# One row per partition of w_down's second part, loaded in four transfers behind wo

## The chip, the cores and the metric

The kernel runs on one core of one Trainium2 chip. The metric is the time of one execution on the device in microseconds (us); less is better. A comparison takes the median of several executions.

## The reference

One decoding step (one token) of a transformer block in bf16: a layernorm, attention with grouped queries over a long cache, the output projection, a second layernorm and a gated feed-forward network, with two residual additions.

```python
B, Sq, D = 1, 1, 1024
Hq, Hkv, Sk, Dh = 32, 4, 65536, 128
F = 3584
...
def _B_ref(x, w_gate, w_up, w_down):
    return (_gelu(x @ w_gate) * (x @ w_up)) @ w_down

x = A_x
h = x + _A_ref(_layernorm(x, axis=-1), A_k_cache, A_v_cache, A_wq, A_wo)
h2 = h + _B_ref(_layernorm(h, axis=-1), B_w_gate, B_w_up, B_w_down)
```

`_A_ref` multiplies by wq, takes the softmax of the scaled scores against k_cache, sums v_cache with it, and multiplies by wo. The caches hold 2 x 64 MB, the weights some 38 MB, and each byte is used once, for a single token.

## The kernel before

The program streams 173 MB through a ring of four slots in SBUF (`ring`, 32 KB per partition and slot). All large transfers are issued by SP, in the order in which the program lists them: wq in two halves (slots 0 and 1), then for each of eight steps (four key-value heads, two halves of the sequence) two K pieces of 4 MB (slots 2 and 3) and one V piece of 8 MB (slots 0 and 1), then wo (8 MB, slots 2 and 3), w_gate (7 MB, slots 0 and 1), w_up (7 MB, slots 2 and 3), and w_down (7 MB, slots 0 and 1). A transfer into a slot waits until PE is done with what the slot held: wo for the last score matmul (`done`), gate for the last matmul on V (`s_step`), up for the matmuls on wo, w_down for those on gate. These waits stand on SP; what SP has issued is worked off by 16 DMA engines in order.

The order is written out by a small recorder, `Flow`. `op` notes an engine's instruction with the tiles that it reads (`r`) and writes (`w`), `dma` a transfer, and `issue` (line 76) emits all of them with the semaphore waits that these need; so most instructions of the profile have line 95 or 91. `dma` returns the count that a semaphore has when the transfer has landed (16 more for each transfer); with `inc` it is left to the reader to wait for that count. The loop over the attention steps on PE (lines 415 to 449) stands apart from it.

w_down has F = 3584 rows of 1024 numbers (2048 bytes). The first P x FA = 2048 rows are its first part, 16 rows on each of 128 partitions (`wa`, slot 0). The other 1536 rows are its second part, FB = 12 rows per partition (`wb`, slot 1), loaded in three pieces of 8, 3 and 1 rows per partition. `parts` lists the four pieces with the semaphore and the count that PE waits for: `r_sem[0]` for the first part, `r_sem[1]`, `k_sem[0]` and `k_sem[1]` for the three pieces. A row per partition is used by eight matmuls of 128 columns (`down`, line 590), whose stationary operand is one column of the activations `actz`. All of them add into two banks, which hold h as their starting value. Ahead of the first part and ahead of the second part's first piece, `stay_busy(4)` runs four matmuls on data that is thrown away (line 598). After the last matmul, DVE and ACT copy the two banks (lines 607 and 608), and SP stores the output (line 609).

Of the kernel before, what the change touches and what calls it, by code (L numbers as in the profile page):

```python
# [11 lines left out]
BF16 = mybir.dt.bfloat16  # L12
# [4 lines left out]
class Flow:  # L17
# [13 lines left out]
    def op(self, e, call, r=(), w=(), after=(), wait=(), inc=None, dma=False, rows=None, **kw):  # L31
        i = len(self.ops)
        deps = {}

        def need(j, hard):
            o = self.ops[j]
            if o["e"] == e and not dma and not o["dma"] and (e == "pe" or not hard):
                return
            deps[j] = True

        for k in r:
            if k in self.writer:
                need(self.writer[k], True)
        for k in tuple(w) + tuple(after):
            if k in self.writer:
                need(self.writer[k], True)
            for j in self.readers.get(k, ()):
                need(j, False)
        if e == "pool":
            if self.rows[0] != rows and self.rows[1] is not None and not self.ops[self.rows[1]]["inc"]:  # L50
                deps[self.rows[1]] = True
            self.rows = rows, i
        last = {}
        for j in deps:
            o = self.ops[j]
            k = j if o["dma"] else o["e"]
            last[k] = max(last.get(k, j), j)
        deps = last.values()
        for k in r:
            self.readers.setdefault(k, []).append(i)  # L60
        for k in w:
            self.writer[k] = i
            self.readers[k] = []
        self.ops.append(dict(e=e, call=call, kw=kw, deps=sorted(deps), wait=wait, inc=inc, dma=dma))
# [44 lines left out]
def kernel(  # L109
# [14 lines left out]
    P = 128  # L124
    D = A_x.shape[-1]
# [4 lines left out]
    F = B_w_gate.shape[1]  # L130
# [28 lines left out]
    def sb(name, shape, dtype=F32):  # L159
        return const.tile(shape, dtype, name=name)  # L160
# [9 lines left out]
    def over(offset, shape, dtype=F32):  # L170

        n = 1
        for x in shape:
            n *= x
        if dtype == F32:
            v = kt_bytes[:, offset // 4:offset // 4 + n]
        else:
            v = kt_bytes[:, offset // 4:offset // 4 + n // 2].bitcast(BF16)
        if len(shape) == 2:
            v = v.rearrange("p (a b) -> p a b", a=shape[0])  # L180
        return v

    def slot(i, n=1):
        return ring[:, i * CW:(i + n) * CW]

    f = Flow(nc, tc)
# [5 lines left out]
    r_sem = [tc.alloc_semaphore("r_landed_%d" % i) for i in range(3)]  # L192
# [306 lines left out]
    FA = CW // D  # L499
    FB = FC - FA  # L500
    at_ps = bank[6][:]
    wv = slot(2, 2).rearrange("p (c n) -> p c n", c=Hq)
    f.dma("sp", wv, A_wo.rearrange("(p c) n -> p c n", p=P), w=["R2", "R3"], wait=done, sem=r_sem[2])
    for c in range(Hq):
        for s in range(DS):
            q = 2 * (c % 2) + s
            op("pe", "matmul", r=["o2z", "R2", "R3"], w=["B6"], out=at_ps[32 * q:32 * q + 32, :], lhsT=o2z[:, c, :],
               rhs=wv[:, c, :].rearrange("k (p s c) -> k s p c", s=DS, c=C4)[:, s], start=(c < 2), stop=(c >= Hq - 2), tile_position=(0, 32 * q))
# [62 lines left out]
    actz = over(16384, [FC, 2 * AZ + 2], BF16)  # L571
# [4 lines left out]
    FZ = 4  # L576
    wa = slot(0)[:, 0:FA * D].rearrange("p (e n) -> p e n", e=FA)
    wb = slot(1)[:, 0:FB * D].rearrange("p (e n) -> p e n", e=FB)
    wb_src = B_w_down[P * FA:F, :].rearrange("(p e) n -> p e n", p=P)
    parts = [(wa, 0, FA, f.dma("sp", wa, B_w_down[0:P * FA, :].rearrange("(p e) n -> p e n", p=P), after=["R0"], inc=(r_sem[0], 16)), r_sem[0])]  # L580
    e0 = 0
    for i, z in enumerate((FB - FZ, FZ - 1, 1)):
        part = wb[:, e0:e0 + z, :]
        s = (r_sem[1], k_sem[0], k_sem[1])[i]
        parts.append((part, FA + e0, z, f.dma("sp", part, wb_src[:, e0:e0 + z, :], after=["R1"] if i == 0 else [], inc=(s, 16)), s))
        e0 += z
# [3 lines left out]
    def down(a_row, w_row):  # L590
        for j in (0, 4, 1, 5, 2, 6, 3, 7):
            q, m = divmod(orow[j], 32)
            nc.tensor.matmul((d_ps, d_odd)[q // 2][32 * q:32 * q + 32, :], lhsT=a_row[:, AZ - m:AZ - m + 32], rhs=w_row[:, j * OB:(j + 1) * OB],
                             start=False, stop=False, skip_group_check=True, tile_position=(0, 32 * q))

    def stay_busy(n):
        for i in range(n):
            nc.tensor.matmul(bank[5][:], lhsT=qs[:, 0, 0, 0:P], rhs=qs[:, 1 + i % 3].rearrange("p s c -> p (s c)")[:, 0:NB], start=True, stop=True)

    with tc.tile_critical(no_gpsimd_drain=True):  # L600
        for w_rows, a0, n, at, sem in parts:
            stay_busy({0: 4, FA: 4}.get(a0, 0))
            nc.tensor.wait_ge(sem, at)
            for e in range(n):
                down(actz[:, a0 + e, :], w_rows[:, e, :])
    h2 = sb("h2", [P, 2, OB], BF16)
# [33 lines left out]
```

## Time and profile before

| | |
|---|---|
| median of 3 runs | 409.87 us (409.83 to 410.06) |
| profiled execution, its own time | 409.71 us |
| its span, first to last instruction | 407.8 us |
| mean granted TensorE clock | 0.778 |
| PE, DVE, ACT, POOL busy | 58%, 50%, 10%, 5% of the span |
| wo: issued, last landing | 329.99, 353.82 us |
| w_gate: issued, last landing | 343.84, 370.76 us |
| w_up: issued, last landing | 360.48, 387.72 us |
| w_down, first part: issued, last landing | 377.01, 397.44 us |
| w_down, second part, three pieces: last landings | 402.34, 404.19, 404.81 us |

Times within the profile count from the start of the span; the profiled execution's own time is 1.9 us longer than its span. Engines are PE (matmul), PEld (its weight loads), DVE, ACT, POOL and SP; a q behind the name is the engine's sequencer, which waits and issues. A row of the timeline has its start, its length, the engine, the line, the operation, what it writes and reads, the count, and in brackets the idle time of the engine before it and what ended that. A row of the table by stretches has the stretch, its length, PE's busy time and matmuls, the granted share of the clock, the busy share of the DMA engines, and GB/s. The trace also holds each DMA packet (start, duration, bytes, queue), without the engine's number, and each increment of a semaphore by a DMA: for a transfer of 128 partitions 16 of them, one from each DMA engine. A transfer has landed with the last of these.

### The profile page before, as it was taken

Reading aid. Unit: us, or ns where it says so; the run is one execution under the profiler, and the core shown is the slowest. Engines: PE = TensorE matmul, PEld = TensorE weight load, DVE = VectorE, ACT = ScalarE, POOL = GpSimd, SP = SyncE. Lnnn points to the kernel's source line nnn. Section 1 sums busy time; section 2 is a strip of 40 time slices with the busy share of each in tenths; the row PEclk is TensorE's granted clock in tenths of the full one; section 3 lists DMA queues with packets and bytes.
Section 4 is the critical chain, followed back from the end, with each engine's and each line's share of the span. In section 5 each row is a group of like instructions: output and inputs, shape, how many; then the busy total and the mean of one; then the engine's idle time right before and its main releaser. Section 6 shows DMA issues by size and latency. Waiting matters only on the chain. (4 is left out here: it accounts for less than half of the span.)

```text
span 407.8 us, 3909 instructions
## 1 busy us (share of the span) xinstructions
PE 234.8 (58%) x1645; PEld 105.8 (26%) x1647; DVE 202.5 (50%) x174; ACT 39.5 (10%) x141; POOL 19.2 (5%) x39
## 2 busy tenths in 40 slices
PE   0433855585577368734973686557465747365376
PEld 0211322232232133212321232223132223142324
DVE  1218860876089328924781687089508941010210
ACT  1000003000300300030003000300220021000000
POOL 4210000001000000010000001000000000012000
PEclk9955995599569967978796689689976976565668
DMA  8999999999999999999998999999999999999995
GB/s 344 427 421 452 415 460 411 460 418 412 453 460 418 411 425 488 418 408 421 476 437 376 453 424 444 421 460 418 411 453 466 418 418 424 452 440 435 399 413 220
DMA packets 4815, 173.12 MB, mean 424 GB/s; under 512 B 580, under 2 KB 584, under 8 KB 840
## 3 DMA queue, kind: packets, MB, share of 16 engines
q1 hardware_dynamic: 4760, 173.02, 98.5%
q8 instruction: 5, 0.08, 0.1%
q14 instruction: 2, 0.02, 0.0%
q10 hardware_dynamic: 48, 0.00, 0.0%
HBM read 173.02 MB, written 0.00 MB: 424 GB/s over the span
## 5 line engine op out<-in xcount | busy, mean ns | idle before, releaser
L95 DVE STREAM_TRANSPOSE ktb<-ring 128x4096 f32<-128x4096 f32 x32 | 141.1, 4418 | 83.4 <-DMA ring<-in_A_k_cache_dram 83.4
L427 PE MATMUL bank<-ktb,qs 128*128 128x512 bf16 x512 | 132.6, 418 | 61.3 <-PEq L413 61.3
L427 PEld LDWEIGHTS bank<-ktb,qs 128*128 128x128 bf16 x512 | 51.5, 104 | 139.2 <-issue 93.6
L439 PE MATMUL bank<-ring,pt 128*32 128x512 bf16 x512 | 46.3, 541 | 36.5 <-PEq L413 36.5
L95 ACT ACTIVATE pt<-sc,nb 128x256 bf16<-128x256 f32 x64 | 31.5, 494 | 255.3 <-DVE nb L95 255.3
L439 PEld LDWEIGHTS bank<-ring,pt 128*32 128x32 bf16 x512 | 19.4, 131 | 60.2 <-issue 57.3
L95 DVE STREAM_TRANSPOSE sc<-bank 128x512 f32<-128x512 f32 x32 | 22.2, 695 | 24.6 <-PE bank L427 24.6
L95 PE MATMUL bank<-ring,xz 128*32 128x512 bf16 (+1 forms) x192 | 19.2, 587 | 17.2 <-DMA ring<-in_B_w_gate_dram 5.2
L95 DVE TENSOR_REDUCE mx<-sc 128x8 f32<-128x1536 f32 (+1 forms) x16 | 19.5, 1219 | 0.5
L95 DVE STREAM_TRANSPOSE ktb<-bank 128x512 f32<-128x512 f32 (+1 forms) x6 | 4.0, 672 | 31.3 <-PE bank L95 30.9
L95 POOL COPY qs<-qsel 32x128 bf16<-32x128 bf16 x16 | 7.8, 490 | 231.4 <-PE bank L427 216.8
L95 PEld LDWEIGHTS bank<-ring,xz 128*32 128x32 bf16 x192 | 7.5, 141 | 26.9 <-issue 15.9
L95 ACT ACTIVATION_READ_ACCUMULATOR pt<-sc,nb 128x1 f32 x64 | 12.0, 187 | 0.0
L448 PE MATMUL bank<-sel,acc_sb 128*128 128x8 f32 x64 | 8.2, 255 | 6.2 <-PEq L413 6.2
L431 PE MATMUL bank<-ident_f,mx 128*8 128x128 f32 x8 | 2.2, 269 | 14.6 <-PEq L413 14.6
L448 PEld LDWEIGHTS bank<-sel,acc_sb 128*128 128x128 f32 x64 | 7.7, 191 | 10.0 <-issue 10.0
L95 PE MATMUL bank<-ring,ktb 128*32 128x512 bf16 x64 | 6.4, 586 | 5.9 <-DMA ring<-in_A_wo_dram 5.9
L95 ACT COPY acc_sb<-bank 128x512 f32<-128x512 f32 x8 | 4.7, 586 | 48.9 <-PE bank L439 48.9
L95 DVE TENSOR_TENSOR h_col<-bank,x_col 128x8 f32<-128x8 f32 x1 | 0.2, 167 | 14.8 <-PE bank L95 14.8
L95 PE MATMUL bank<-sel,ktb 128*128 128x16 f32 (+1 forms) x24 | 5.2, 356 | 3.5 <-DVE bank L95 2.7
L95 POOL MEMSET ktb<- 128x1024 bf16 (+2 forms) x3 | 3.5, 1164 | 75.8 <-PE bank L427 75.8
L433 PE MATMUL bank<-diag,ones_f 8*128 8x8 f32 x16 | 3.7, 299 | 5.7 <-PEq L413 5.7
(85 smaller groups left out, 60.9 us busy)
## 6 DMA issues: line engine op xcount, KB each, us to landing
ring<-in_A_k_cache_dram SPq DMA_DIRECT2D x16, 4096.0 KB, 24.9
ring<-in_A_wq_dram SPq DMA_DIRECT2D x2, 4096.0 KB, 16.7
ring<-in_B_w_gate_dram SPq DMA_DIRECT2D x1, 7168.0 KB, 26.9
ring<-in_B_w_up_dram SPq DMA_DIRECT2D x1, 7168.0 KB, 27.2
ring<-in_B_w_down_dram SPq DMA_DIRECT2D x1, 4096.0 KB, 20.4
ring<-in_B_w_down_dram SPq DMA_DIRECT2D x1, 2048.0 KB, 25.0
ring<-in_B_w_down_dram SPq DMA_DIRECT2D x1, 768.0 KB, 25.9
ring<-in_B_w_down_dram SPq DMA_DIRECT2D x1, 256.0 KB, 26.0
```

Source lines behind the costliest of these rows:

```text
L95: ins = getattr(self.eng[e], o["call"])(**o["kw"])
L427: m = nc.tensor.matmul(bank[c][:], lhsT=qs[:, jt].rearrange("p s c -> p (s c)")[:, s * P:(s + 1) * P], rhs=mv[:, :, J, :, u], start=(s == ...
L431: nc.tensor.transpose(out=mxT_ps, in_=mx1[:], identity=ident_f[:]).then_inc(s_step, 1)
L433: nc.tensor.matmul(bc_ps, lhsT=ones_f[0:rep, :], rhs=diag[:], start=True, stop=True).then_inc(s_step, 1)
L439: m = nc.tensor.matmul(acc[32 * q:32 * q + 32, :], lhsT=pt[:, c, n, :, :].rearrange("p h s -> p (h s)"), rhs=v_sb[:, c, :, n, :], start=(c ...
L448: m = nc.tensor.matmul(o_ps, lhsT=acc_sb[:, u * Dh:(u + 1) * Dh], rhs=sel[:, u:SQ:NS], start=(u == 0), stop=(u == NS - 1))
```

## The change

One of the twelve rows per partition of w_down's second part (the first, `wb_src[:, 0]`) goes into a tile of its own, `c_row`, in four transfers of 25, 25, 64 and 14 partitions. They are issued by SP right behind wo and ahead of gate, wait for nothing (the tile is used for nothing else), and count on `r_sem[1]`. The first piece in the ring then has 7 rows instead of 8, and the piece's wait on PE covers the four transfers too, since it waits for the count of all that was issued on `r_sem[1]`. PE runs the eight matmuls of the row in `c_row` behind that wait, ahead of the seven.

```diff
     f.dma("sp", wv, A_wo.rearrange("(p c) n -> p c n", p=P), w=["R2", "R3"], wait=done, sem=r_sem[2])
+    wb_src = B_w_down[P * FA:F, :].rearrange("(p e) n -> p e n", p=P)
+    c_row = sb("c_row", [P, 1, D], BF16)
+    for p0, p1 in ((0, 25), (25, 50), (50, 114), (114, P)):
+        f.dma("sp", c_row[p0:p1], wb_src[p0:p1, 0:1, :], inc=(r_sem[1], 16))
     for c in range(Hq):
...
     wb = slot(1)[:, 0:FB * D].rearrange("p (e n) -> p e n", e=FB)
-    wb_src = B_w_down[P * FA:F, :].rearrange("(p e) n -> p e n", p=P)
     parts = [(wa, 0, FA, f.dma("sp", wa, B_w_down[0:P * FA, :].rearrange("(p e) n -> p e n", p=P), after=["R0"], inc=(r_sem[0], 16)), r_sem[0])]
-    e0 = 0
-    for i, z in enumerate((FB - FZ, FZ - 1, 1)):
+    e0 = 1
+    for i, z in enumerate((FB - FZ - 1, FZ - 1, 1)):
...
         for w_rows, a0, n, at, sem in parts:
-            stay_busy({0: 4, FA: 4}.get(a0, 0))
+            stay_busy({0: 4, FA + 1: 4}.get(a0, 0))
             nc.tensor.wait_ge(sem, at)
+            if a0 == FA + 1:
+                down(actz[:, FA, :], c_row[:, 0, :])
             for e in range(n):
                 down(actz[:, a0 + e, :], w_rows[:, e, :])
```

## The prediction

> **What bounds the kernel now.** I read four views in this order: the page's first three parts, the DMA issues, the PE timeline of the last 12 us, and the granted clock in that stretch. The page's slices of DMA time and its queue table come first:
>
> ```profile
> DMA  8999999999999999999998999999999999999995
> ...
> q1 hardware_dynamic: 4760, 173.02, 98.5%
> ...
> HBM read 173.02 MB, written 0.00 MB: 424 GB/s over the span
> ```
>
> The 16 DMA engines are busy in 98.5% of the span, from the first slice to the last. SP issues gate at 343.84, up at 360.48 and w_down at 377.01 us, each while the transfer before it is still moving (wo lands at 353.82, gate at 370.76, up at 387.72). There is no hole into which the moved rows could go: the change moves no byte less, and what it moves ahead delays gate, up and the first part of w_down by its own time.
>
> The end, in the timeline of PE and of the two copies:
>
> ```profile
> 397.48 3.40 PE L593 MATMUL bank<-ring,ktb 128*32 128x128 bf16 x128
> 401.05 0.81 PE L598 MATMUL bank<-qs 128*128 128x512 bf16 x3 [0.16 <-issue]
> 402.38 0.62 PE L593 MATMUL bank<-ring,ktb 128*32 128x128 bf16 x30 [0.53 <-DMA ring<-in_B_w_down_dram]
> 403.50 1.65 PE L593 MATMUL bank<-ring,ktb 128*32 128x128 bf16 x66 [0.49 <-issue]
> ...
> 404.85 0.12 PEld L593 LDWEIGHTS bank<-ring,ktb 128*32 128x32 bf16 x8 [0.28 <-DMA ring<-in_B_w_down_dram]
> 405.34 0.26 ACT L608 CAST h<-bank 64x128 bf16<-64x128 f32 x1 [26.20 <-PEq L600]
> 405.34 0.28 DVE L607 CAST h<-bank 64x128 bf16<-64x128 f32 x1 [9.89 <-PEq L600]
> 405.71 0.35 SPq L609 DMA_DIRECT2D out_dram<-h  x1
> ```
>
> PE waits for each of the three pieces of w_down's second part, and its last eight matmuls start when the last piece has landed; 0.5 us later the copies run. So **the last landing sets the end**, and a landing is complete only when the slowest of 16 DMA engines is. The trace's landing events, one for each engine, show how uneven these are (us):
>
> ```
> last piece of w_down, 16 engines:
> 402.97 403.09 403.09 403.10 403.14 403.17 403.24 403.32
> 403.35 403.47 403.76 404.29 404.51 404.65 404.67 404.81
> ```
>
> Ten engines are done by 403.47; five are 0.8 to 1.3 us behind them. The trace shows where the lag begins. Packets of the kind "instruction" (16 KB at 33.22, 358.00, 376.88 and 401.08 us, about 1.0 us each; 8 KB at 99.83 and 143.25, 0.3 us each) each sit on one engine, and from each on one more landing lags by 0.4 to 1.4 us and never catches up. The trace does not number the engines, so **which of the 16 lag is the unknown of this case.**
>
> **The change, step by step.** Data packets have these durations: 2048 B takes 84 ns (median of 128), 6144 B 234, 16384 B 615, 32768 B 1213; a 4 B completion mark 9 ns.
>
> 1. *Taken off the second part.* Its first piece has eight packets per engine, which shrink from 16384 to 14336 B. On the line between 6144 and 16384 B (381 ns for 10240 B), a packet goes from 615 to 539 ns: 8 x 0.076 = 0.61 us less on every engine.
>
> 2. *Added behind wo.* 128 packets of 2048 B, unevenly spread. Rows on how: transfers of 128 partitions have 16 landings; x_in's 32 partitions give 16 marks behind 32 packets, two each; the output's four rows give one landing event at 406.17 and four more at 406.86 to 406.90, that is four engines with a row each. All splits are even. Kept even, 64 rows are four on each of 16 engines and 14 rows one on each of 14. For 25 the ends are all 25 on one engine and two on most of them; even and between them is five on each of five, and that I take, with both transfers on the same five. The five then get 5+5+4+1 = 15 rows, nine get 5, two get 4. With marks: 15 x 0.084 + 4 x 0.009 = 1.30 us on the five, 5 x 0.084 + 0.018 = 0.44 on the nine, 4 x 0.084 + 0.009 = 0.35 on the two.
>
> [...]
>
> 3. *Net at the last landing.* The five: +1.30 - 0.61 = +0.69 us. The nine: -0.17. The two: -0.26.
>
> 4. *The queue.* SP issues wo at 329.99 and is free until gate at 343.84; four issues at 0.33 to 0.88 us each (the four of w_down span 2.24) end near 333. They wait for nothing of their own, wo is already ahead of them in each engine's queue, and the engines are busy with V until 334.47. Cost nothing, with ten microseconds of cover.
>
> 5. *What moves in between.* Gate, up and w_down's first part land 0.35 to 0.44 later where the lagging engine is outside the five. The next transfer is issued when PE has finished the one before (377.01, nearly 9 us before up begins to land at 385.85), so a shift of 0.44 opens no hole. The matmuls and the layernorm shift with their data: PE is 0.44 later at the start of w_down.
>
> 6. *PE at the end.* The eight matmuls per row are the same 224, with the row of the new tile ahead of the other seven; no instruction more. The wait at r_sem[1] now covers five transfers; behind it stand the last 96 matmuls and the copies. The four matmuls that keep PE busy then reach from 396.79 into the half-clock stretch, where two or three of them take 0.43 instead of 0.22, so the first part's matmuls start near 398.1 instead of 397.48 (the data lands at 397.88). About 92 of them run at 27 ns until 400.54 and 36 at 14 ns, to 401.1; with the 0.4 and four times 0.22 that follow, PE is ready near 402.3. The first piece lands at 402.34 - 0.17 = 402.17. So the 0.5 us by which PE was ahead there are used up, but not more: 64 matmuls with the 0.5 idle that the timeline shows among them end near 404.0, when the next piece lands (404.02), and the last lands at 404.64.
>
> **Sum**: the last landing goes from 404.81 to 404.64, the copies and the output follow: -0.17 us. The profiled execution took 409.71 us around a span of 407.8, so it would take 409.54; it lies 0.16 under the median of the runs shown, 409.87, which gives 409.70. I forecast **409.7 us**, within 0.2% (0.82 us, about what a measurement of this kernel can tell from no change).
>
> **The rivals.**
>
> *A lagging engine is among the five* (chance 0.22). Then it lands 0.69 later than now. The five laggards end at 404.29, 404.51, 404.65, 404.67 and 404.81, so the last landing would be 404.98 to 405.50: slower by 0.17 to 0.69, 410.0 to 410.6. It decides from one such engine on. [...]
>
> *The memory side of each engine is what is full* (0.10). Every engine moves 32768 B in 1213 ns, 27.0 GB/s, all alike; no row says whether that limit is the engine's or that of the partitions it writes. If it is the partitions', the moved rows cost the same time wherever they are queued: 128 x (84 - 76) / 16 = 0.06 us plus marks, 409.95.
> [...]
>
> *PE becomes the bound* (0.08): slower. The clock in the last stretches:
>
> ```profile
> 397.13:400.54 3.41, 3.41 (x118) 0.50 0.93 396
> 400.54:403.95 3.41, 2.23 (x90) 1.00 0.74 294
> ```
>
> Full clock comes after a stretch in which PE was busy throughout. If a 0.44 to 1.3 us later start leaves that stretch short of full, the half clock lasts on: the first part's 128 matmuls end at 401.5, the four fillers take 1.7 instead of 0.9 and end at 403.6, 64 matmuls at 27 ns reach 405.3 and the last 32 406.2, where now they end near 405.0: +1.2 us, 411.1. In an execution whose clock already falls so, the end is PE's today (405.5) and the change costs 0.6. It decides when the clock after 400.5 is half.
>
> *All 25 rows on one engine* (0.04): the change doesn't spread as meant. That engine gets 55 rows, 4.6 us, -0.61: +4.0. Not a laggard (403.0 to 403.5), it would land near 407.3: 412.4.
>
> **How the numbers follow.** Forecast 0.50 (409.6 to 409.8), the four rivals 0.44, something else 0.06. The forecast's error is mostly one of sign, and all but two cases stay inside 0.2%. Faster by over 0.2% would need four times what can be taken off the laggards: 0.04 for what I do not see. Slower by over 0.2%: all of the single-engine case, half of PE's, and a little of the first: 0.10. Within: 0.86. The range from 409.5 to 410.6 holds the forecast, the laggard among the five and the memory side, and leaves out most of the last two.
>
> **What would show it.** In the changed kernel's landing events, c_row's second 25 rows should have five late events and the others at once; the first piece's packets should take 539 ns; gate should land 0.35 to 0.44 later (1.3 if a laggard is in the five); the last piece's slowest landing should come 0.17 before that of now, with ten landings spread up to 404.2. The forecast is wrong if the last landing moves later, if PE's eight last matmuls no longer start at the landing, or if the clock after 400.5 us is half.

## The result, and the profile after

The changed kernel takes 411.23 us (median of 8 runs, 411.03 to 411.59) against 409.91 us of the kernel before (8 runs, 409.74 to 410.06): a ratio of 1.0032, 95% interval 1.0022 to 1.0043. It is **slower by 1.3 us**, where 0.2 us less was forecast. The profiled execution is the slowest of the eight, 411.59 us with a span of 409.6.

The page shows nothing of it: the DMA engines' share is the 98.5% of before, and the rate falls by 2 GB/s.

```profile
DMA  8999999999999999999999998999899999999995
...
q1 hardware_dynamic: 4928, 173.02, 98.5%
...
HBM read 173.02 MB, written 0.00 MB: 422 GB/s over the span
```

The timeline of PE, with the first copy as its last row, has more:

```profile
355.20 6.11 PE L95 MATMUL bank<-ring,ktb 128*32 128x512 bf16 x64 [6.72 <-DMA ring<-in_A_wo_dram]
373.12 5.21 PE L95 MATMUL bank<-ring,xz 128*32 128x512 bf16 x64 [6.50 <-DMA ring<-in_B_w_gate_dram]
399.70 2.62 PE L596 MATMUL bank<-ring,ktb 128*32 128x128 bf16 x128
402.25 1.04 PE L601 MATMUL bank<-qs 128*128 128x512 bf16 x4
403.99 0.30 PE L596 MATMUL bank<-c_row,ktb 128*32 128x128 bf16 x8 [0.70 <-DMA ring<-in_B_w_down_dram]
404.11 0.50 PE L596 MATMUL bank<-ring,ktb 128*32 128x128 bf16 x22
405.80 1.12 PE L596 MATMUL bank<-ring,ktb 128*32 128x128 bf16 x66 [1.18 <-issue]
407.10 0.28 DVE L612 CAST h<-bank 64x128 bf16<-64x128 f32 x1 [10.12 <-PEq L603]
```

The matmuls on wo and on gate in the kernel before:

```profile
353.95 6.44 PE L95 MATMUL bank<-ring,ktb 128*32 128x512 bf16 x64 [5.89 <-DMA ring<-in_A_wo_dram]
370.89 6.03 PE L95 MATMUL bank<-ring,xz 128*32 128x512 bf16 x64 [5.19 <-DMA ring<-in_B_w_gate_dram]
```

The surprise is the first row after the change: the matmuls on wo start at 355.20, where before they started at 353.95. wo was issued ahead of the four transfers and lands 1.25 us later all the same (355.07 against 353.82). Gate's slowest landing is at 372.99 instead of 370.76, and w_down's first part starts 2.2 us later. The last piece lands at 406.43 instead of 404.81 (+1.62), and the copies start at 407.10 instead of 405.34 (+1.76). Idle time of 1.18 us, marked "issue", stands inside the second part's matmuls; before, it was 0.49.

The landing events give the loss as a mean over the 16 DMA engines: V's last transfer +0.04, wo +0.49, gate, up and w_down's first part +2.19 each, the last two pieces +1.60. So the four transfers cost 2.19 us per engine where the forecast had 0.35 to 1.30 (0.70 in the mean), and the row that the ring no longer loads gave back 0.59, where it had 0.61.

The packet records show where the 2.19 us are. A packet of 2048 B took 84 ns in the kernel before; of the 128 behind wo, 79 now take over 100 ns, up to 196, and they sum to 15.4 us instead of 10.8. Large packets that run beside them are stretched: wo's last ones from 2.42 us to up to 3.41 (3.4 us more in sum than before), gate's first ones from 2.12 to up to 3.48 (15.4 us more). Together these are 34 us, 16 times 2.1.

### The profile page after: what moved, and what is told of

Read it like the earlier page. It is cut to its first block, busy times and chain, and to the rows that moved or that the text cites. A ratio compares the mean times of both kernels' runs of the same rounds, so it can differ in the third digit from the quotient of the medians.

```text
span 409.6 us, 3915 instructions
## 1 busy us (share of the span) xinstructions
PE 229.9 (56%) x1647; PEld 104.0 (25%) x1647; DVE 202.5 (49%) x174; ACT 39.5 (10%) x141; POOL 19.3 (5%) x39
## 3 DMA queue, kind: packets, MB, share of 16 engines
q1 hardware_dynamic: 4928, 173.02, 98.5%
## 5 line engine op out<-in xcount | busy, mean ns | idle before, releaser
L427 PE MATMUL bank<-ktb,qs 128*128 128x512 bf16 x512 | 130.7, 414 | 64.8 <-PEq L413 64.8
L95 PE MATMUL bank<-ring,xz 128*32 128x512 bf16 (+1 forms) x192 | 17.3, 539 | 18.8 <-DMA ring<-in_B_w_gate_dram 6.5
```

Of the source, the lines that this page charges most:

```text
L95: ins = getattr(self.eng[e], o["call"])(**o["kw"])
L427: m = nc.tensor.matmul(bank[c][:], lhsT=qs[:, jt].rearrange("p s c -> p (s c)")[:, s * P:(s + 1) * P], rhs=mv[:, :, J, :, u], start=(s == ...
```

## The experiments

Three theories of the loss were left by this. **Foreign partitions**: a row takes longer, and holds up large packets of other engines, where the engine that writes it is not the one that writes the same partitions in the large transfers. **Uneven load**: five engines with 15 rows each hold up the rest. **Small or many transfers**: 2 KB packets, or four transfers instead of one, cost that much in any form. Which engine writes which partition no trace tells: a packet's record has neither. The kernels below were laid out by an assumption of the author's about it. The counts of foreign rows in the expectations (115 in the changed kernel, 120, 64) and the price of 0.21 us for each rest on this assumption, and no run shows them. The runs show which partitions each transfer wrote, how the row was divided, and what that cost.

### The same row in one transfer, and in four even ones

```diff
-    for p0, p1 in ((0, 25), (25, 50), (50, 114), (114, P)):
+    for p0, p1 in ((0, P),):
```

> The row goes into its tile behind wo as one transfer of 128 partitions instead of four. In the changed kernel gate's 16 landings came 2.19 us later in the mean than before, where 128 packets of 84 ns are 0.67 us for each of 16 engines. Theory of the foreign partitions (a row costs some 0.2 us more when an engine writes partitions that another engine writes in the large transfers; a transfer of 128 partitions has none of these): gate's mean landing +0.7 us against before, no large packet stretched, the last landing within 0.1 us of before's 404.81, time within 0.1% of before (409.8 to 410.2). Theory of uneven loads (the five engines with 15 rows): the same, since all engines get eight rows. Theory of small packets or of an early row (2 KB packets behind wo cost 2 us in any form): gate +2.2 us, the end +1.6 us, 411.2.

Measured: 410.24 us, ratio 1.0012 (1.0002 to 1.0021). Gate's mean landing +0.63 us, no 2 KB packet above 94 ns, the last landing +0.11. So an early row in small packets costs no more than the packets' own time (128 x 84 ns are 0.67 us for each engine), and the third theory falls for packets. The 0.4 us by which the time still rose are taken up further down.

```diff
-    for p0, p1 in ((0, 25), (25, 50), (50, 114), (114, P)):
+    for p0, p1 in ((0, 32), (32, 64), (64, 96), (96, P)):
```

> [...] Theory of the foreign partitions: 115 such rows cost 24 us of engine time in the changed kernel, 0.21 us each; 120 of them give 25 us, so gate's mean landing is +2.2 to 2.3 us, the last landing +1.6 us, 411.2 to 411.6, and large packets of gate are stretched. Theory of uneven loads: even, so gate +0.7 us and the time within 0.1% of before. Theory of the number of transfers (four instead of one): as the changed kernel, 411.2.

Measured: 411.48 us, 1.0041 (1.0027 to 1.0055); gate +2.10 us (V's last transfer, ahead of the rows, is already 0.24 late in this profile), 2 KB packets up to 248 ns, wo's up to 3.58 us. The load is even if 32 rows go two to each engine, as x_in's do (16 marks behind 32 packets), and the loss is near that of the changed kernel: the theory of uneven load falls. In the two kernels' timelines PE's first matmuls on wo and on gate tell it at a glance. One transfer of 128:

```profile
354.02 5.46 PE L95 MATMUL bank<-ring,ktb 128*32 128x512 bf16 x64 [7.64 <-DMA ring<-in_A_wo_dram]
371.63 4.66 PE L95 MATMUL bank<-ring,xz 128*32 128x512 bf16 x64 [7.22 <-DMA ring<-in_B_w_gate_dram]
```

Four of 32:

```profile
355.32 5.87 PE L95 MATMUL bank<-ring,ktb 128*32 128x512 bf16 x64 [7.09 <-DMA ring<-in_A_wo_dram]
373.14 3.18 PE L95 MATMUL bank<-ring,xz 128*32 128x512 bf16 x32 [7.06 <-DMA ring<-in_B_w_gate_dram]
```

Starts are to be compared, not the idle times before them, which also hold how early PE was done with what came before. The views end near 376 us and cut rows on gate off in length and count, here and in the next section.

### The same rows, to partitions below 64 and to those above

```diff
+    wb_src = B_w_down[P * FA:F, :].rearrange("(p e) n -> p e n", p=P)
+    c_row = sb("c_row", [P, 1, D], BF16)
+    for s0 in (0, 32):
+        for r in range(4):
+            p0 = s0 + r
+            f.dma("sp", c_row[p0 + 0:p0 + 0 + 29:4], wb_src[p0:p0 + 29:4, 0:1, :], inc=(r_sem[1], 16))
```

This is added to the kernel before, with the second part left whole in the ring. The second kernel has `c_row[p0 + 64:p0 + 64 + 29:4]` instead, and the same source; its expectation sets it against the first.

> Against the kernel before, 64 rows more are loaded behind wo in eight transfers of eight partitions each, four apart, into a tile that no one reads; nothing is taken out of the second part. [...] Theory of the foreign partitions: no stretching, 8 x 84 ns + 8 x 9 ns = 0.74 us on eight engines and nothing on the others, gate's mean landing +0.37 us; the last landing +0.74 if a lagging engine is among the eight, else 0. Time +0.0 to +0.75 us. Theory of uneven loads: as badly as 64 rows of the changed kernel, mean +1.1 us. Theory of the number of transfers: twice as many as in the changed kernel, so gate +2 us or more.

> [...] Only the destination's partitions differ. Theory of the foreign partitions: 64 x 0.21 = 13 us of engine time more than in that run, gate's mean landing +0.37 + 0.83 = +1.2 us, large packets of gate stretched, the time 0.6 to 1.2 us above that run's. Theories of uneven loads, of small packets and of the number of transfers: the same time as that run within 0.1%.

Measured: partitions below 64, 410.66 us, 1.0018 (1.0009 to 1.0027); those from 64 on, 411.41 us, 1.0035 (1.0022 to 1.0049). Gate's mean landing is +0.48 and +1.43 us, the last landing +0.87 and +1.88. The 64 packets take 84 to 86 ns in the one and up to 175 in the other, where wo's packets reach 3.32 us. Source, number, shape and size of the transfers are the same; in the program only the partitions written differ. That the same engines carry them was assumed; no record numbers the engines. The times alone would separate the two kernels less well: the 11 runs of the first spread from 409.85 to 411.39 us, which no run here explains, the five of the second from 411.06 to 411.75. The packets and landings of the profiles make the difference plain. Partitions below 64 first, then those from 64 on:

```profile
354.05 5.28 PE L95 MATMUL bank<-ring,ktb 128*32 128x512 bf16 x64 [7.91 <-DMA ring<-in_A_wo_dram]
371.79 4.67 PE L95 MATMUL bank<-ring,xz 128*32 128x512 bf16 x48 [7.51 <-DMA ring<-in_B_w_gate_dram]
```

```profile
354.98 5.08 PE L95 MATMUL bank<-ring,ktb 128*32 128x512 bf16 x64 [8.53 <-DMA ring<-in_A_wo_dram]
372.79 3.61 PE L95 MATMUL bank<-ring,xz 128*32 128x512 bf16 x36 [7.61 <-DMA ring<-in_B_w_gate_dram]
```

wo, ahead of all of these rows in the queue, lands on time in the first and a microsecond late in the second. Eight small transfers to partitions below 64 run at the packets' own time and leave wo where it was (354.05 against 353.95): the third theory falls for their number too. What the program changes between the two is the partitions written, and these make the difference. That it is because other engines write them in the large transfers fits both runs if the layout was assumed rightly; no run shows it.

### The row in two transfers

```diff
-    for p0, p1 in ((0, 25), (25, 50), (50, 114), (114, P)):
+    for p0, p1 in ((0, 64), (64, P)):
```

> [...] Theory of the foreign partitions, now with the price from the four runs so far (0.21 us of engine time for each foreign row, by 115 of them in the changed kernel): gate's mean landing +0.67 + 64 x 0.21 / 16 = +1.5 us against before, halfway between the one transfer (+0.63) and the four of 32 partitions (+2.10); the last landing +0.9 us; time 410.7 to 411.1. Theory that one transfer is free because it is a single one: two cost little more than one, gate +0.7 us, 410.3.

Measured: 411.44 us, 1.0035 (1.0025 to 1.0045); gate +1.87, the last landing +1.48. The cost is there, but is not halfway between one transfer (+0.63) and four of 32 (+2.10), as the first theory here expected. Worked out from the mean landings less 0.69 to 0.71 us for the packets and their marks, each of the 128 rows cost 0.15 us of engine time more ((1.87 - 0.69) x 16 / 128), against 0.19 in the changed kernel and 0.17 in the four of 32 (0.14 without the 0.24 by which V was late there). How many pieces the 128 rows go in hardly matters here, once it is more than one: less the shift of V's last transfer, gate is 1.86 to 1.90 us late with two transfers, with the four of 32, and with the change's four in two further profiles below (2.15 in the changed kernel's own). What sets the cost was not settled. Two transfers to the two halves of the partitions do worse than one transfer: 411.44 us against 410.24.

### Which engines lag

```diff
-            f.dma("sp", c_row[p0 + 0:p0 + 0 + 29:4], wb_src[p0:p0 + 29:4, 0:1, :], inc=(r_sem[1], 16))
+            f.dma("sp", c_row[p0 + 0:p0 + 0 + 17:4], wb_src[p0:p0 + 17:4, 0:1, :], inc=(r_sem[1], 16))
```

Here the transfers to partitions below 64 have five rows each instead of eight (the lines against the kernel with eight). Split evenly, as the changed kernel's rows are by the increments, they load five engines with eight rows each.

> [...] Nothing is stretched, so gate's landings tell which engines these are: five of 16 come 8 x 84 + 8 x 9 ns = 0.74 us later than before, eleven don't. If no lagging engine is among the five (as the forecast had it): the slowest landing of gate stays near 370.8, the last landing near 404.8, the time within 0.1% of before. If the slowest one is among them (the run with eight engines moved it by 0.87): gate's slowest landing is at 371.5, the last landing at 405.5, time 410.4 to 410.6.

Measured: 410.01 us, 1.0005 (0.9996 to 1.0014). Gate's 16 landings, before and here:

```
before: 368.91 368.93 369.02 369.04 369.07 369.08 369.10 369.12 369.18 369.28 369.30 369.40 369.71 370.24 370.63 370.76
here:   368.94 368.99 369.07 369.11 369.15 369.16 369.18 369.20 369.26 369.69 369.73 369.77 370.31 370.46 370.76 370.81
```

The first group shrinks from twelve to nine: three undisturbed engines moved by 0.6 to 0.7 us. The other two of the five are, as far as the rows can be paired, the two that have lagged since the instruction packets of 99 and 143 us: they had 353.09 and 352.68 for wo in this run, and with the 16.94 us of gate and 0.74 are due at 370.77 and 370.36. The slowest engine is not among the five in this execution, though by the +0.89 on the slowest gate landing it seems to be among the eight in that run's.

### The stop inside the second part's matmuls

```diff
+    for i in range(28):
+        op("pe", "matmul", r=["ident_bf"], w=["B5"], out=bank[5][0:32, 0:8], lhsT=ident_bf[:, 0:32], rhs=ident_bf[:, 0:8], start=True, stop=True)
+
     AZ = 31
```

Put into the kernel with one transfer, into the kernel before, and into the changed kernel.

> The run with one transfer of 128 partitions, and 28 matmuls of 8 columns on the identity, thrown away, put on PE ahead of up's matmuls, where PE waits some five us for data. They move PE's later instructions by 28 places. In all profiles so far PE stops at the 31st matmul of the second part, after an instruction packet, and goes on 6.0 to 6.3 us after the start of the first part's matmuls, whatever has landed; with one transfer that is 0.4 us too late for the last landing. Theory that this stop is the fetch of PE's instructions: it comes 28 matmuls earlier, at the second part's start, goes by while PE waits there, and the copies start 0.5 us behind the last landing again: time within 0.1% of before, 0.3 to 0.4 us less than the one transfer without the 28 (409.8 to 410.0). Theory that the 0.4 us are the matmuls' or the transfer's own: no change, 410.2.

> The kernel before with the same 28 matmuls ahead of up's, as the control. In before's profile the stop ends at 403.50 us and its matmuls are done by the time the last piece lands (404.81), so with or without them the landing sets the end: 409.7 to 409.9, no change beyond 0.1%. If the stop costs before something too: up to 0.2 us less.

> The changed kernel with the 28 thrown-away matmuls ahead of up's, which took PE's stop in the second part away in the run with one transfer. In the changed kernel's profile the last landing is 1.62 us later than before and the copies 1.76. Theory of two costs (the writes to other engines' partitions set the landing, the stop adds what is left): the landing stays 1.6 us late, the copies start 0.5 us behind it, the time falls by 0.1 to 0.3 us, to 410.9 to 411.1. Theory that the stop is most of the loss: the time falls by a us or more, to near 410.

Measured: one transfer 409.84 us, 1.0001 (0.9991 to 1.0010), where it was 410.24; the kernel before 409.82, 0.9998 (0.9989 to 1.0007); the changed kernel 410.91, 1.0028 (1.0017 to 1.0039), where it was 411.23. The end of the timeline with one transfer, without the 28 matmuls:

```profile
402.78 0.50 PE L596 MATMUL bank<-ring,ktb 128*32 128x128 bf16 x22
404.48 1.13 PE L596 MATMUL bank<-ring,ktb 128*32 128x128 bf16 x66 [1.20 <-issue]
...
405.79 0.28 DVE L612 CAST h<-bank 64x128 bf16<-64x128 f32 x1 [10.85 <-PEq L603]
```

and with them:

```profile
403.09 0.95 PE L599 MATMUL bank<-ring,ktb 128*32 128x128 bf16 x56
...
404.30 0.91 PE L599 MATMUL bank<-ring,ktb 128*32 128x128 bf16 x32 [0.25 <-DMA ring<-in_B_w_down_dram]
...
405.40 0.28 DVE L615 CAST h<-bank 64x128 bf16<-64x128 f32 x1 [10.28 <-PEq L606]
```

The last landings are 404.93 and 404.87. Without the 28, PE stops after 30 matmuls and runs the last 66 without waiting for a landing, so the copies come 0.86 us after the last landing; with them 56 run in one piece, PE waits for the landings, and the copies come 0.53 after it, as before. That the stop is the fetch of PE's instructions is inferred from two things. In each of the nine profiles that have it, an instruction packet starts 2.3 to 2.5 us ahead of its end. And with 28 instructions more ahead of it, this packet starts 1.9 us after the first part's matmuls instead of 3.8 (400.02 - 398.15 against 402.02 - 398.20, one transfer), and the stop is gone from its place. It ends 6.0 us after the start of the first part's matmuls in the kernel before (403.50 - 397.48), 6.1 in the changed kernel and 6.3 with one transfer, whatever has landed.

### The four transfers alone

```diff
+    wb_src = B_w_down[P * FA:F, :].rearrange("(p e) n -> p e n", p=P)
+    c_row = sb("c_row", [P, 1, D], BF16)
+    for p0, p1 in ((0, 25), (25, 50), (50, 114), (114, P)):
+        f.dma("sp", c_row[p0:p1], wb_src[p0:p1, 0:1, :], inc=(r_sem[1], 16))
```

Added to the kernel before, with the second part left whole in the ring.

> The kernel before with the change's four transfers (25, 25, 64, 14 partitions) added behind wo, into a tile that no one reads; the second part stays whole in the ring. The price of the four transfers alone. If the changed kernel's loss is their price less the row that the ring no longer loads (0.6 us): gate's mean landing +2.2 us, as there, the last landing +2.2, the time 412.0 to 412.2. If part of the loss comes from the shorter piece or from the row's place in PE's order: less, 411.3 to 411.9.

Measured: 411.61 us, 1.0039 (1.0025 to 1.0052); gate's mean landing +1.85, and +1.85 at every later one. The time is that of the second expectation, but not for its reason: gate is loaded ahead of the shorter piece and used ahead of the row's matmuls, so neither can have held it up in the changed kernel. Rather, the price of the transfers differs between profiles: in the changed kernel with the 28 matmuls, which also come behind gate, it is at +1.88 too, where the changed kernel itself had +2.19. With that price the sum holds: 1.88 less 0.61 is the +1.27 that its last piece shows.

## Why the prediction was wrong

- **What bounds the kernel** was right: the last landing sets the end before, and there is no hole in the DMA engines' time.
- **Step 1**, the row taken off, held: 0.59 us against 0.61, and the first piece's packets take 539 ns as forecast.
- **Step 2 is the step that failed**, by its price. The split was right: the semaphore of the new tile has three increments at the issue and 56 single ones, which is 5 + 5 + 16 + 14 engines for the row and 16 for the first piece. But 84 ns for a row came from a transfer of 128 partitions. In one transfer of 128 behind wo the row cost the mean engine 0.63 us; in the changed kernel's four it cost 2.19 instead of 0.70.
- **Step 3**, the net at the last landing, follows: -0.17 on the laggards became +1.62.
- **Step 4** took "wo is already ahead of them in the queue" for cover. The queue's order did not hold across the engines: the first of the 128 packets starts at 351.59 us, and 125 of them start before wo's last landing at 355.07. So rows were written while other engines still worked on wo, and wo landed 1.25 us later. That they went into those engines' partitions is the first theory's reading, which no run shows.
- **Step 5** had no hole opening, which held; the shift that it passes on was 2.2 us instead of 0.44.
- **Step 6** took the idle 0.5 us among the last matmuls as a fixed length. It is a stop that ends 6.0 to 6.3 us after the first part's matmuls start, in the profiles of the kernel before, of the changed kernel and with one transfer. A row moved ahead of the first part delays these and shortens what follows, so the stop and the 66 matmuls behind it outlast the landings. That costs 0.4 us with one transfer (410.24 against 409.84). In the changed kernel it is 0.14 by the profiles (the copies come 0.67 us after the last landing, and 0.53 with the 28 matmuls) and 0.3 by the medians (411.23 against 410.91), whose intervals overlap.
- **The rivals.** The memory side asked whether the partitions written set a limit. By the two kernels with eight transfers they matter, but its size was wrong: it took the work there as merely kept, 0.06 us, where the changed kernel's mean engine paid 1.49 us more than the packets' own time. A laggard among the five: by the pairing of the landings two of the five engines with transfers of five rows are laggards, though not the slowest. That the change's five are the same engines no run shows, nor in which order small transfers take the engines. If they are, the one since 99 us, which ends at 404.29 in the kernel before, would with +0.69 be at the 404.98 with which this rival's range begins, and the forecast's -0.17 would without the stretched packets have been +0.17. PE's rival came true in part, and through another door than the clock, which is full from 401.1 us on in the changed kernel. All 25 rows on one engine fell, by the five increments.

Of the 1.3 us, 1.0 to 1.2 is thus the landing (1.1 by 410.91 against 409.82, with the 28 matmuls in both) and 0.1 to 0.3 PE's stop. No version here beats the kernel before; one transfer with the stop moved equals it.

## What to carry to other kernels

Beside large transfers a row in small transfers can cost several times its packets' own time, part of it on transfers issued earlier: here gate landed 2.19 us later for 0.70 us of packets, and wo, issued ahead of them, 1.25 us later. Neither bytes nor rows per engine told it: 128 rows cost gate 0.63 us in one transfer and 1.87 in two of 64, and 64 rows 0.48 us to partitions below 64 and 1.43 to those from 64 on. So measure a split with the partitions that its pieces write. While the engines are full (98.5% of the span here), try all 128 partitions in one transfer first: at 410.24 us it was the cheapest of the divisions of this row. Where the last stage runs close behind its data, look for a stop in the profile that nothing releases, and find out what it counts from before shortening the wait next to it.

## What the runs showed of the hardware

- A row of 2048 B cost 0.14 to 0.27 us of engine time in all beyond its own 84 ns and the marks, where the 128 rows went in two or four transfers or 64 rows went to partitions from 64 on (mean landings of six profiles), and single large packets were stretched by up to 1.4 us (2.12 to 3.48). In one transfer of 128 it cost nothing beyond them (gate +0.63 us, the packets alone 0.67), and in eight transfers to partitions below 64 it cost 0.03 us (gate +0.48 us, where 0.37 is the packets and marks). Why is not shown.
- An instruction packet is followed by one more landing that lags by 0.4 to 1.4 us for the rest of the run, in which all transfers queue without a gap. In the kernel before, the last of the 16 landings of a K piece is 0.41 us behind the first at 32 us, ahead of the 16 KB packet at 33.22, and 1.81 us behind it at 42 to 44; at the last piece, 405 us, it is 1.84.
- 28 matmuls of 8 columns in a stretch where PE waits moved a stop of PE out of the last stage. They saved 0.4 us with one transfer, where the stop ended last, 0.1 to 0.3 in the changed kernel, and nothing in the kernel before, where a landing did (409.82 against 409.84).
